# A fused attention and SwiGLU kernel: integer weight conversion in fewer steps, the first batch's attention in token halves, quarter sums used where they are made, and a new order for the first stretch

## The chip, the cores and the metric

The kernel runs on one core of a Trainium2 chip. The metric is the device time of one execution in microseconds (us); the median of several runs is taken.

## The reference

Eight batches of 512 tokens and 32 states of width 512 (8 heads of 64) read each other by attention; the 544 rows of each batch then go through a feed-forward block with RMS norm and gated SiLU.

```python
# x: (8, 8, 512, 64), state: (8, 8, 32, 64), both float32
scores = 1/sqrt(D) * x @ state.T          # (B, H, 512, 32)
xread  = softmax(scores, -1) @ state      # tokens read the states
scores2 = 1/sqrt(D) * state @ x.T         # (B, H, 32, 512)
sread  = softmax(scores2, -1) @ x         # states read the tokens
x = concat(xread, sread)                  # -> rows (B * 544, 512)
xn = x / sqrt(mean(x * x, -1) + 1e-6) * rms_g
g, val = xn @ w_gate, xn @ w_val          # 512 -> 1536
out = (g * sigmoid(g) * val) @ w_out      # 1536 -> 512
```

`moe_rms_g` and the three weights come as they are made by `setup_inputs()`: the weights are float64 (a float32 array times a float64 scalar), so that each value has 8 bytes in the chip's memory and the kernel makes a float32 out of it on the chip.

## The kernel before, in words

**Layout.** Batches run one after the other. Batch 0 works while the weights arrive and is done plainly; batches 1 to 7 use a scheme of seven products for the hidden layer (`hidden_seven`, L842) and, twice nested, for the output (`project_twice`, L1146), whose sums of weights and of quarter weights are made once. The states' rows of all batches come last.

**Weights.** They come in 18 raw pieces of 128 x 1024 doubles (1 MB), three for each of six pairs `mp` of hidden blocks: gate, value and output columns. `load_piece` puts a piece into a buffer of the pool `raws` (4 buffers, `RAW_AHEAD`), by SP's queue; when a piece has been converted, the load of the one four further on is issued. ScalarE makes the exponent of each value in three steps (`exponents`: L246, L249, L252). VectorE makes the mantissa in two (`values`: L273, L276) and multiplies the two in a third (L282), in 1024 columns a step. The first piece is done in two parts. The finished gate and value weights lie in one of three buffers `w_sb` and are stored to memory for later batches (`fetch` brings them back).

**Batch 0's attention.** `first_half` and `second_half` handle 256 tokens each, in two chunks of 128 tokens. The state is transposed (L463) into `apart`, where a head pair has its two heads in separate columns. `chunk_scores` transposes x (L499, four 128x128 transposes a chunk), copies it (L501), makes the scores (L504) and the softmax's maximum, difference and exponential (L510 to L514). `half_read` sums the exponentials (L522), divides, transposes (L532), copies to `aT_s` (L535), multiplies by the state's Gram matrix (`gram`, made at L475 and L479) to get each token's square sum (L543), sums that over partitions by matmuls (L548), takes the power -1/2 on GpSimd (`mean_root`, L299), spreads the result over rows (`along_rows`, L306 and next) and scales `aT_s` (L558). Tokens are read by value weights: `own_weights` (L695) multiplies the scaled state by a pair's weights to `v`, so that the hidden layer of a token is `v` times `aT_s` (`hidden`, L738; two matmuls for each of gate and value, 512 columns). `states_read` with `state_scores` (L568) is the other direction. `project_as_ready` (L945) is the output product of batch 0.

**Batch 1's attention** (`tokens_read`, from L328) begins while batch 0 runs.

**Quarter sums.** `weight_sums` (L988) makes sums of the output weights. `weight_quarters` (L1100) makes of each of seven outer blocks three quarter sums `w2` (pool of three buffers) and one in place, 128 x 384 each, stores them, and `fetch_quarters` brings them back (576 KB) for each use, also for the first one, in batch 1. Four steps a block; blocks 2, 3, 6 in batch 0 (stream Q), 0, 1, 4, 5 in batch 1 (stream q).

**PSUM pools.** `aps`, `vps`, `fx` with two banks each, `fy` and `fz` with one.

**Order.** Each part of the work is a generator that yields after each step. A string names the generators in the order in which their next step is issued; each engine takes its instructions in that order, and semaphores do the rest. `ORDER` (400 letters) is batch 0 with the beginnings of batch 1, `FIRST` is batch 1, `PERIOD` batches 2 to 6, `LAST` batch 7, `STATES` the states' rows. The letters of `ORDER`: a, b the two halves; s the states of batch 0; A, S batch 1's two reads; e exponents, d values; v `own_weights`; h, t, u hidden products, SiLU and gate of batch 0; p, c projection and its stores; w, k, Q first products of batch 1, weight sums, quarter sums; z a matmul on the identity (`keep_awake`, L1281: one call is one matmul of 256 columns, which counts as two instructions), 16 of them, of which most stand in the first 75 letters.

Of the kernel before, what the change touches and what calls it, by code (L numbers as in the profile page):

```python
# [20 lines left out]
RAW_AHEAD = 4  # L21
W_BUFS = 3
FLAT = 1793.0

ORDER = (
    "zzzaaazazbabaaabdebdbadeabeazszbbeadebeezdzbazzaabbaszeabbazzddbebeaaezbddabddsa"
    "eAbzAAdaeasAbAaeAvsavvbaAdsdAdsAhdtdAhehudpdpeedthdeededdevupddvevpddAeehdeddteh"
    "dAAAdeheuAAdeSSedhddpvAtudAdeAAvvpdphhdAshAAteshAueepdetpSedesAeddAdedpsdduddsde"
    "psvevvdedpAhsddeedddtheeeAedehvsvuvAeAhddpddtpAduedpheAAdAedAehdAhtSddSAdevvdvuA"
    "phhtAdheSudAheAtAtdphkkuSkAkkkkuAkSSASkwkpSwQsQwpQppwwpskSQpcQkSQScpcQQwQcwwQwQQ"  # L30
# [10 lines left out]
    "vaaahahatthhqxthaxuqhahutthtxuhquuqhtahqhaauqahluvtvuhhhtquxqqqhttqxuhqxquhxqufx"  # L41
    "hhtahqtuqahhxuthaautsahahuuhtGahtvuauthkaahuxauhuhxtshhuautgxuahkhtuGthtkhuuuhuu"
    "khutppushpuupukapkkkppkkcakpppcpkkfpkkGppagkpppppaapsaakpkpckfpapkfkckasokppaaaa"
    "kpsscskpappapkpgpppgksskagaoppkcagppksaakppkaapwpkpspskskwoxkwxkxppxpfxokglcopsc"
    "foxsoo"
# [14 lines left out]
def kernel(  # L60
# [49 lines left out]
    HS = S // 2  # L110
    QM = HM // 2
# [12 lines left out]
    def load_state(b):  # L124

        rows[b] = two.tile([P, 2, D], F32, name="rows")
        for e in range(2):
            nc.sync.dma_start(out=rows[b][:, e], in_=state[b, e::2])

    def load_x(b, *queues):  # L130
# [5 lines left out]
        x_sb[b] = (one if b else x_0).tile([P, NC, H * D], F32, name="x_b")  # L136
        for c in range(NC):
            (queues or (nc.sync,))[c % max(1, len(queues))].dma_start(
                out=x_sb[b][:, c].rearrange("p (h d) -> p h d", h=H),
                in_=x[b, :, P * c:P * c + P, :].rearrange("h p d -> p h d"))  # L140

    ident = consts.tile([P, P], F32, name="ident")
# [9 lines left out]
    for i, bound in enumerate((-896.0 - 7.5 / 16, 1.0, 255.0 * 128, 1e-6)):  # L152
        GE.memset(bounds[:, i:i + 1], bound)
    rms_g = consts.tile([P, NI], F32, name="rms_g")

    groups = consts.tile([P, 4, Ns], F32, name="groups")
    for i in range(4):
        GE.tensor_copy(groups[:, i], ident[:, 0:Ns])
        for j in range(1, 4):
            GE.tensor_tensor(out=groups[:, i], in0=groups[:, i],  # L160
                             in1=ident[:, Ns * j:Ns * j + Ns], op=ALU.add)


    apart = x_0.tile([P, 4, 2, Ns], F32, name="apart")
    GE.memset(apart, 0.0)
    blocks = x_0.tile([P, P], F32, name="blocks")
    GE.memset(blocks, 0.0)
    for j in range(4):
        GE.memset(blocks[Ns * j:Ns * j + Ns, Ns * j:Ns * j + Ns], 1.0 / DM)
# [10 lines left out]
    for mp in range(NM // 2):  # L180
        for dram in (moe_w_gate, moe_w_val):
            pieces.append(dram[:, 2 * P * mp:2 * P * mp + 2 * P].rearrange("(i p) f -> p i f", p=P))
        pieces.append(
            moe_w_out[2 * P * mp:2 * P * mp + 2 * P].rearrange("(m p) f -> p m f", p=P))
# [12 lines left out]
    def home(k):  # L197

        mp, kind = divmod(k, 3)
        if kind == 2:  # L200
            return wo[:, 2 * mp:2 * mp + 2].rearrange("p m (i f) -> p m i f", f=P)
        return (w_sb[mp] if kind else new_w(mp))[:, :, :, kind, :]

    def load_parts(k):

        src = pieces[k] if k < len(pieces) else None
        if src is None or src.dtype == F32:
            return
        raw[k] = raws.tile([P, 8 * P, 2], I32, name="raw")
        out_ = raw[k].rearrange("p (a f) two -> p a (f two)", a=src.shape[1])  # L210
        for a in parts(k):
            nc.sync.dma_start(out=out_[:, a], in_=src[:, a].bitcast(I32))
# [6 lines left out]
    def parts(k):  # L219

        n = pieces[k].shape[1]
        return (slice(0, n // 2), slice(n // 2, n)) if k == 0 else (slice(0, n),)

    exs = {}

    def columns(k, a):
        n = pieces[k].shape[1]
        return slice(8 * P * a.start // n, 8 * P * a.stop // n)  # L230

    def exponents():
# [3 lines left out]
        for k in range(len(pieces)):  # L236
            for a in parts(k):
                if k not in raw:
                    yield from range(3)
                    continue  # L240
                if a.start == 0:
                    exs[k] = conv.tile([P, 8 * P], I16, name="ex")
                    lin = conv.tile([P, 8 * P], F32, name="lin")
                ex, line = exs[k][:, columns(k, a)], lin[:, columns(k, a)]
                half = raw[k][:, columns(k, a)].bitcast(I16)[:, :, 3::4]
                SE.activation(out=line, in_=half, func=ACTF.Prelu, scale=1.0 / 16,  # L246
                              bias=bounds[:, 0:1], alpha=1.0 / FLAT)
                yield
                SE.activation(out=ex, in_=line, func=ACTF.Prelu, bias=bounds[:, 1:2],  # L249
                              alpha=FLAT)  # L250
                yield
                SE.activation(out=ex.bitcast(U16), in_=ex, func=ACTF.Relu, scale=128.0,  # L252
                              bias=bounds[:, 2:3])
                yield

    def values():
        for k in range(len(pieces)):
            for a in parts(k):
                if a.start == 0:
                    to = home(k)  # L260
                    if k in raw:
                        top_ = conv.tile([P, 8 * P], I32, name="top")
                dst = to[:, a]
                if k not in raw:
                    src = pieces[k].rearrange("p a (c f) -> p a c f", f=P)
                    for i in range(a.start, a.stop):
# [1121 lines left out]
```

## Time and profile before

| | |
|---|---|
| median of 3 runs | 745.59 us (744.95 to 745.7) |
| span of the profiled execution | 742.6 us; of it the profile shows no other total, so the span is its own time, 3.0 us under the median of the runs |
| TensorE (PE) | 735.6 us busy, 5582 matmuls |
| VectorE (DVE) | 579.0 us |
| ScalarE (ACT) | 380.2 us |
| GpSimd (POOL) | 260.3 us |
| DMA | 146.15 MB, mean 197 GB/s |

The profile takes one execution by the hardware's profiler. Busy time is the time in which an engine executed; a share that is near the whole span says that this engine has little idle time left, and where it has any must be looked up by stretch. The chain of waits follows the work that ended last back to the start: each piece begins where the one that released it ended. A row of a group gives line, engine, operation, tiles and shapes, then the number of instructions, the busy time in us, the mean of one in ns, and the idle time of the engine just before them with what ended it.

### The profile page before, as it was taken

What the parts mean: (1) busy time and instruction counts of PE and PEld (TensorE: products, weight loads), DVE (VectorE), ACT (ScalarE), POOL (GpSimd) and SP (SyncE); (2) the same over time, 40 slices, a digit from 0 to 9 for tenths busy, and PEclk for the clock granted to TensorE, in tenths of its full rate; (3) what the DMA queues carried; (4) which work ended last, traced back from release to release, by engine and by line L of the source; (5) the groups of instructions that cost most, each with busy time, mean ns of one, the idle gap of its engine ahead of it and who ended that gap; (6) DMA issues with size and microseconds to landing.
All of it is one profiled execution on the core that took longest, in us unless ns stands there. A gap on an engine that the chain in (4) does not pass through costs nothing.

```text
span 742.6 us, 14225 instructions
## 1 busy us (share of the span) xinstructions
PE 735.6 (99%) x5582; PEld 591.0 (80%) x5582; DVE 579.0 (78%) x957; ACT 380.2 (51%) x635; POOL 260.3 (35%) x362
## 2 busy tenths in 40 slices
PE   8999999999999999999999999999999999999998
PEld 6534444779977998789878997799778987899996
DVE  4999978899856994699659985799469955798862
ACT  5999972573265725472366426562556336511220
POOL 3100004341283128512573228312841267324400
PEclk9999999999999999999999999999999999999999
DMA  9987936964783278608881669328860883063411
GB/s 296 274 294 274 398 118 223 309 245 148 239 304 105 90 285 283 195 1 297 228 304 23 226 213 315 98 95 292 274 188 6 317 230 127 1 223 117 135 52 28
DMA packets 60994, 146.15 MB, mean 197 GB/s; under 512 B 14848, under 2 KB 31744, under 8 KB 54016
## 3 DMA queue, kind: packets, MB, share of 16 engines
q1 hardware_dynamic: 47808, 125.78, 48.9%
q10 hardware_dynamic: 13120, 19.47, 9.2%
q8 instruction: 44, 0.72, 0.4%
q14 instruction: 22, 0.18, 0.1%
HBM read 116.46 MB, written 28.77 MB: 196 GB/s over the span
## 4 chain that ended last, share of the span: by engine, by line
PE 98%; ACT 1%; DMA 1%; DVE 0%; SPq 0%; issue 0%; DVEq 0%
PE f L842 40%; PE f L1146 31%; PE f L945 6%; PE pv L738 6%; PE pv L695 3%; PE at L695 3%; PE f L1008 2%; PE at L631 1%; PE at L355 1%; PE at L437 1%; DMA rows<-in_state_dram 1%; PE f L1281 0%; PE pv L504 0%; PE at L306 0%; PE at L499 0%; PE at L649 0%
## 5 line engine op out<-in xcount | busy, mean ns | idle before, releaser
L842 PE MATMUL f<-aT_s,v 128*128 128x256 f32 x504 | 118.8, 381 | 0.0
L842 PEld LDWEIGHTS f<-aT_s,v 128*128 128x128 f32 x504 | 94.8, 191 | 19.2 <-DVE h L1200 4.2
L905 DVE TENSOR_TENSOR g<-g,f 128x512 f32<-128x512 f32 x84 | 55.8, 684 | 58.6 <-PE f L842 45.7
L842 PE MATMUL f<-aT_t,vs 128*128 128x256 f32 x336 | 86.6, 381 | 0.0
L1174 POOL TENSOR_TENSOR kept<-kept 128x256 f32<-128x256 f32 x28 | 20.9, 746 | 183.2 <-DVE kept L1186 116.9
L1159 ACT COPY kept<-f 128x512 f32<-128x512 f32 (+1 forms) x56 | 30.1, 538 | 105.8 <-PE f L1146 99.8
L1146 PE MATMUL f<-w,h 128*128 128x128 f32 x588 | 74.7, 276 | 0.0
L842 PEld LDWEIGHTS f<-aT_t,vs 128*128 128x128 f32 x336 | 63.0, 190 | 12.5 <-issue 3.5
L1146 PEld LDWEIGHTS f<-w,h 128*128 128x128 f32 x588 | 69.8, 192 | 1.1 <-DVE h L1200 0.8
L722 POOL TENSOR_TENSOR vs<-v 128x256 f32<-128x256 f32 x42 | 31.0, 737 | 109.8 <-ACT v L707 109.6
L896 ACT ACTIVATE hb<-g 128x1024 f32<-128x1024 f32 x42 | 44.4, 1058 | 46.8 <-DVE g L905 43.1
L299 POOL TENSOR_TENSOR ri<-ss,mhalf 128x4 f32<-128x4 f32 (+1 forms) x9 | 9.4, 1045 | 126.9 <-issue 82.0
L918 DVE TENSOR_TENSOR hb<-hb,f 128x512 f32<-128x512 f32 (+1 forms) x48 | 31.1, 649 | 28.8 <-PE f L842 28.7
L945 PE MATMUL f<-wo,hb 128*128 128x512 f32 x96 | 44.0, 599 | 0.0
L738 PE MATMUL pv<-aT_s,v 128*128 128x512 f32 x96 | 43.8, 598 | 0.0
L842 PE MATMUL f<-aT_t,v 128*128 128x256 f32 x168 | 43.8, 383 | 0.0
L842 PE MATMUL f<-aT_s,vs 128*128 128x256 f32 x168 | 43.3, 380 | 0.0
L1146 PE MATMUL f<-wo,h 128*128 128x128 f32 x336 | 42.3, 275 | 0.0
L1146 PE MATMUL f<-wo,hb 128*128 128x128 f32 x336 | 42.1, 275 | 0.0
L918 DVE TENSOR_TENSOR hb<-hb,c 128x512 f32<-128x512 f32 (+1 forms) x48 | 35.7, 743 | 6.5 <-ACT hb L896 6.1
L1146 PEld LDWEIGHTS f<-wo,hb 128*128 128x128 f32 x336 | 40.3, 192 | 0.4
L1146 PEld LDWEIGHTS f<-wo,h 128*128 128x128 f32 x336 | 39.8, 192 | 0.0
(227 smaller groups left out, 1639.9 us busy)
## 6 DMA issues: line engine op xcount, KB each, us to landing
w_m<-w_d SPq DMA_DIRECT2D x48, 1024.0 KB
w<-t_d SPq DMA_DIRECT2D x49, 576.0 KB
out_dram<-kept SPq DMA_DIRECT2D x28, 256.0 KB
raw<-in_moe_w_val_dram SPq DMA_DIRECT2D x6, 1024.0 KB
raw<-in_moe_w_out_dram SPq DMA_DIRECT2D x6, 1024.0 KB
w_d<-w_m SPq DMA_DIRECT2D x6, 1024.0 KB
x_b<-in_x_dram SPq DMA_DIRECT2D x6, 1024.0 KB
x_d<-xB ACTq DMA_DIRECT2D x6, 1024.0 KB
```

Of the source, the lines that this page charges most:

```text
L695: TE.matmul(out=pv[e][Ns * j:Ns * j + Ns, :], lhsT=stT_g[b][D * e:D * e + D, j, :], rhs=w[D * e:D * e + D, j].rearrange("p m k f -> p (m k ...
L722: GE.tensor_tensor(out=vs[:, 0], in0=a21, in1=a22, op=ALU.add)
L738: TE.matmul(out=to[0], lhsT=lhs(i, k), rhs=r, start=(i == 0), stop=(i == len(rhs) - 1))
L842: TE.matmul(out=ps[:, i, 0:half], lhsT=l[:, i, :], rhs=r, start=(start and i == 0 and k == 0), stop=(k == len(lhs) - 1), skip_group_check= ...
L896: SE.activation(out=hb[:, 2 * mp:2 * mp + 2, 0:n].rearrange("p m (c t) -> p m c t", c=2), in_=q["g"][:, :, :, 0:half], func=ACTF.Silu if s ...
L905: VE.tensor_tensor(out=to, in0=to, in1=q[ps][:, :, 0:half], op=ALU.add)
L918: VE.tensor_tensor(out=part, in0=part, in1=val, op=ALU.mult)
L945: TE.matmul(out=banks[r], lhsT=hb[:, m, P * r:P * r + P], rhs=wo[:, m, :], start=(m == 0), stop=(m == NM - 1))
L1008: TE.matmul(out=banks[name][:, r, :], lhsT=lhs(k)[:, P * r:P * r + P], rhs=rhs(k), start=(start and r == 0 and k == 0), stop=(k == HM - 1) ...
L1146: TE.matmul(out=to[half][:, slot, :], lhsT=lhs[:, k, :], rhs=rhs[:, k, :], start=(fresh and n in (0, 4) and k == 0), stop=(k == QM - 1), s ...
L1159: SE.copy(of_half(k, i), banks[name][i])
L1174: GE.tensor_tensor(out=k[:, 4:8:3], in0=k[:, 5:6].to_broadcast([P, 2, QD]), in1=k[:, 4:8:3], op=ALU.add)
```

## The change

**Weights as integers.** A raw piece lands 2 bytes behind a word boundary of its tile (`I16` tile with one more double). One 32-bit word then holds the middle of a double: sign, exponent and top of the mantissa come as one 16-bit half, and the rest of what float32 needs lies in one word. ScalarE takes two steps, and gives the sign and exponent bits and the mantissa's top as an int32 (`tops`); VectorE takes two: one `tensor_scalar` (multiply and minimum) on the words, and one bitwise OR that writes the float32's bits. For `mp` 0 the first two pieces hold gate and value of one hidden block each instead of gate of two and value of two. `RAW_AHEAD` is 5.

**Batch 0's attention.** Its x comes in two halves of 256 tokens, two neighbouring tokens on a partition (`load_x_halves`), and its output is stored accordingly. The scores use a wider `apart`; the state is transposed twice, with the head pair swapped the second time. The exponentials are transposed before the division. The matrix `gram` has four more columns that sum the exponentials, so that one matmul gives squares and sums, tokens on partitions; L548 and `along_rows` go from here, and a second set of transposes comes. `of_states` (letter g) makes the state's Gram matrix and scaled state; `rms_g` is loaded as four rows and transposed. `first_own` makes `v` of the first pair of hidden blocks in two parts, and `first_pair` does their hidden products in two halves of 256 tokens.

**Quarter sums.** `early_quarters` (Q, blocks 0 to 2) and `late_quarters` (q, blocks 3 to 6) leave the sums in the buffers from which batch 1 uses them; the seven loads for batch 1 go.

**Order.** `ORDER` has 352 letters and 11 keep-awake steps (z 6, y 5; they run on `wake`, a tile of ones that VectorE fills); `FIRST` is new. The sums `groups` are a stream of their own (i).

```diff
-RAW_AHEAD = 4
+RAW_AHEAD = 5
...
 ORDER = (
-    "zzzaaazazbabaaabdebdbadeabeazszbbeadebeezdzbazzaabbaszeabbazzddbebeaaezbddabddsa"
-    "eAbzAAdaeasAbAaeAvsavvbaAdsdAdsAhdtdAhehudpdpeedthdeededdevupddvevpddAeehdeddteh"
...
+    "zyzaaiayaigaeeaeaaagdaadeddgggzzzbbbbbbaaabzdbeyaaabegvvbabiyayaaebvddaevbavvaae"
+    "bbesbshAhbbdAbbeddsdebbiAAAAhtdvvhvAAhstuudeAthAAsesdsAApsppAApseeeAAAAAeuAhstee"
...
+    def load_x_halves():
+        x_sb[0] = x_0.tile([P, 2, H, HT, D], F32, name="x_b")
+        for i in range(2):
+            for h in (slice(0, H // 2), slice(H // 2, H)) if i == 0 else (slice(0, H),):
+                nc.sync.dma_start(out=x_sb[0][:, i, h].rearrange("p h c d -> p h (c d)"),
+                                in_=x[0, h, HS * i:HS * i + HS, :].rearrange("h (p c) d -> p h (c d)", c=HT))
+            yield
...
     def load_parts(k):
-        raw[k] = raws.tile([P, 8 * P, 2], I32, name="raw")
...
+        raw[k] = raws.tile([P, 8 * P + 1, 4], I16, name="raw")
+        flat = raw[k].rearrange("p f four -> p (f four)")[:, 1:1 + 32 * P]
+        out_ = flat.rearrange("p (n f) -> p n f", n=len(pieces[k]))
...
     def exponents():
-                SE.activation(out=line, in_=half, func=ACTF.Prelu, scale=1.0 / 16,
-                              bias=bounds[:, 0:1], alpha=1.0 / FLAT)
-                SE.activation(out=ex, in_=line, func=ACTF.Prelu, bias=bounds[:, 1:2],
-                              alpha=FLAT)
-                SE.activation(out=ex.bitcast(U16), in_=ex, func=ACTF.Relu, scale=128.0,
-                              bias=bounds[:, 2:3])
+                SE.activation(out=lin[:, c], in_=raw[k][:, c.start + 1:c.stop + 1, 0], func=ACTF.Prelu,
+                              bias=bounds[:, 0:1], alpha=1.0 / FLAT)
+                SE.activation(out=tops[k][:, c], in_=lin[:, c], func=ACTF.Prelu, scale=2.0 ** 19,
+                              bias=bounds[:, 1:2], alpha=FLAT)
...
     def values():
-                    VE.tensor_scalar(top, hi, 0xfffff, 0x100000,
-                                     op0=ALU.bitwise_and, op1=ALU.bitwise_or)
-                    VE.scalar_tensor_tensor(out=man, in0=top, scalar=2.0 ** 32,
-                                            in1=r.bitcast(U32)[:, :, 0], op0=ALU.mult, op1=ALU.add)
-                    VE.scalar_tensor_tensor(out=dst, in0=man, scalar=-2.0 ** -52, in1=ex,
-                                            op0=ALU.mult, op1=ALU.mult)
+                    VE.tensor_scalar(rest, word, 2.0 ** -13, 2.0 ** 19 - 1, op0=ALU.mult, op1=ALU.min)
+                    VE.tensor_tensor(out=dst.bitcast(I32), in0=rest, in1=top, op=ALU.bitwise_or)
...
     def half_read(h):
+        yield from transposed()
+        ge = [f.tile([P, 2, P + 4], F32, name="f") for f in (fy, fz)]
+        for c in range(HT):
+            for i in range(2):
+                TE.matmul(out=ge[c][:, i, :], lhsT=aT[:, i, P * c:P * c + P], rhs=gram[:, i, :],
+                          start=True, stop=True)
...
+        VE.tensor_tensor(out=e, in0=e, in1=z2.rearrange("p c k -> p (c k)").unsqueeze(2).to_broadcast(e.shape),
                          op=ALU.mult)
+        yield from transposed()
...
+    def early_quarters():
+        for o in range(3):
+            yield from quarter_weights(o)
+            nc.sync.dma_start(out=t2_d[o], in_=w2_sb[o])
+            yield
+            if o != 1:
+                yield from last_quarter(o)
...
     def fetches_of_quarters(b):
-        for n in range(7 * (b - 1) + 3, 7 * b + 3):
+        for n in range(7 * (b - 1) + 3 if b > 1 else 7, 7 * b + 3):
...
+    def first_pair():
+        for i in range(2):
+            for m in range(2):
+                for k in range(2):
+                    for e in range(2):
+                        TE.matmul(out=done_[m][k][:, HS * i:HS * i + HS], lhsT=v_sb[0, 0][0][:, e, m, k, :],
+                                  rhs=aT_s[0][:, e, HS * i:HS * i + HS],
+                                  start=(i == 0 and e == 0), stop=(i == 1 and e == 1), skip_group_check=True)
+                yield
...
-    load_x(0, nc.scalar, nc.scalar, nc.sync, nc.sync)
+    nc.scalar.dma_start(out=rms_rows, in_=moe_rms_g.rearrange("(i p) -> i p", p=P))
+    first_x = load_x_halves()
+    next(first_x)
     load_piece(0)
-    load_piece(1)
-    nc.sync.dma_start(out=rms_g, in_=moe_rms_g.rearrange("(i p) -> p i", p=P))
-    for k in range(2, RAW_AHEAD):
+    next(first_x, None)
+    for k in range(1, RAW_AHEAD):
         load_piece(k)
     load_state(1)
     load_x(1)
```

More of the change, by code (lines that the diff above doesn't have):

```diff
@@ L261, in values @@
                     if k in raw:
[L262 removed]
+                        words = raw[k].rearrange("p f four -> p (f four)").bitcast(U32)
+                        words = words[:, 0:16 * P].rearrange("p (f two) -> p f two", two=2)[:, :, 1]
                 dst = to[:, a]
                 if k not in raw:
[L265 to L267 removed]
```

355 lines of the change are left out of this document (210 added, 145 removed).

## The prediction, on record before the changed kernel ran

> **What bounds the kernel now.** I read the page first (busy times), then the chain that ended last, in order of time, then busy times by stretch and the groups of the first 130 us.
>
> ```profile
> span 742.6 us, 14225 instructions
> PE 735.6 (99%) x5582; PEld 591.0 (80%) x5582; DVE 579.0 (78%) x957; ACT 380.2 (51%) x635; POOL 260.3 (35%) x362
> ```
>
> TensorE is busy 99% of the span: the other 7.0 us (742.6 - 735.6) are all that it is idle. So only two things can move the time: less work on TensorE, or fewer moments in which it waits or runs fillers. The next question is where those moments are. The chain in order of time, from its first matmul, and then from the first product of batch 0 (L738) on:
>
> ```profile
> 5.64 0.45 PE at L463
> 6.09 0.85 PE f L1281 x2
> 6.94 0.85 PE at L499 x4
> ...
> 9.50 0.96 PE pv L504 x8
> 10.46 0.44 PE at L499 x4
> ...
> 13.97 0.49 PE f L1281 x2
> 14.46 1.02 PE at L568 x16
> ...
> 17.50 0.49 DVE gram L479 x2
> ...
> 20.09 0.59 ACT aT_s L535
> ...
> 25.04 0.69 DVE eS L543
> ...
> 25.78 1.05 PE f L548 x8
> 26.83 0.27 PE pv L306 x2
> 27.10 0.44 PE at L328 x4
> 27.54 1.02 PE f L695 x16
> ```
>
> ```profile
> 29.87 5.41 PE pv L738 x12
> 35.28 3.43 PE f L945 x8
> ...
> 41.45 3.63 PE f L945 x8
> ...
> 129.62 11.37 PE f L842 x52
> ```
>
> From 29.87 on each piece starts where the one before it ends: 12 + 8 matmuls of 512 columns at 0.43 us, the next, and so on into batch 1. The 0.20 us by which 3.63 exceeds 3.43 follows a packed group (L695, 64x32 tiles; an earlier one stands at 27.54); it is a change of tile shape, not a wait for data. So nothing behind 29.87 waits, and all that can be won in waits lies ahead of it. There the chain passes through VectorE and ScalarE (softmax, norm) and through fillers (L1281, the keep-awake matmuls, 16 steps in the order string). The matrix engine also starts at half pace: four transposes (L499) take 0.85 us at 6.94 and 0.44 us at 10.46.
>
> The other engines in the first stretch, and in batch 1 (128 to 172 hidden products, 172 to 210 projection):
>
> ```profile
> 0.00:100.00 100.00, 96.68 (x492) 48.83 (x493) 83.14 (x121) 89.65 (x113) 8.18 (x37) 1.00 0.86 296
> 128.00:172.00 44.00, 43.95 (x278) 33.90 (x259) 40.59 (x71) 26.75 (x46) 16.49 (x20) 1.00 0.72 246
> 172.00:210.00 38.00, 38.00 (x419) 34.42 (x418) 31.75 (x55) 12.79 (x28) 14.01 (x18) 1.00 0.66 224
> ```
>
> (Columns: length, then busy PE, PEld, DVE, ACT, POOL, granted clock, DMA share, GB/s.) ScalarE at 89.65 of 100 us and the DMA engines at 0.86 are nearly full in the first 100 us; yet they don't hold TensorE up there.
>
> **The change, part by part.**
>
> *Weights as integers.* Per piece of 1024 columns, from the groups of the first 130 us:
>
> ```profile
> L246 ACT ACTIVATE lin<-raw,bounds 128x1024 f32<-128x1024 int16 x17 | 21.2, 1244 | 0.0
> L249 ACT ACTIVATE ex<-lin,bounds 128x1024 int16<-128x1024 f32 x17 | 19.6, 1150 | 0.2
> L252 ACT ACTIVATE ex<-ex,bounds 128x1024 uint16<-128x1024 int16 x17 | 19.5, 1149 | 0.2
> L276 DVE SCALAR_TENSOR_TENSOR raw<-top,raw 128x1024 f32<-128x1024 int32 x17 | 20.8, 1221 | 0.2
> L273 DVE TENSOR_SCALAR top<-raw 128x1024 int32<-128x1024 int32 x17 | 11.6, 682 | 0.0
> ```
>
> ScalarE goes from 1.24 + 1.15 + 1.15 to 1.24 + 1.15: 1.15 less, 18 pieces, 20.7 us. VectorE now takes 0.68 (L273) and two steps of two inputs, 1.22 each (L276; L282 is of the same kind and size); the change leaves a tensor_scalar and an OR of two tensors. The OR has two inputs like L276, so 1.22. The tensor_scalar multiplies and clips 32-bit integers, which no row does; its bounds are 0.68 (L273, one input, same size and stride) and 1.22 (L276). I take 0.68, the same kind of instruction: 1.22 less, 22 us. Both savings fall behind 29.87, where TensorE does not wait: worth nothing there. Ahead of it they shorten two queues, and that is inside the chain below.
>
> *Landing two bytes off.* The raw weights land 2 bytes past a word, so that one 32-bit word holds the middle of each double. No row shows such a transfer; it may cost nothing (a gain has no cause, for the bytes and descriptors are the same) or much. The point from which it costs: in 0 to 100 the DMA share is 0.86, so 14 us are free; the 18.9 MB of weights at 296/0.86 = 344 GB/s are 55 us of that. It may be 14/55, a quarter, slower before the stretch is bound by DMA. I take nothing. The Trainium skill, page "DMA: Bandwidth & Descriptors", section "How a descriptor splits into AXI transactions", says that a run that doesn't start on 256 bytes takes one transaction more; by it a 2 KB row would take 9 for 8, an estimated 12%, and the sum would stay as it is. No run of this kernel shows it.
>
> *Attention of batch 0 in halves.* TensorE loses the sums over partitions (L548, 2 x 1.05) and the rows of the norm (L306, twice 0.27): 2.6. It gains a second set of transposes (8 at 0.11, 0.9), the second state transpose and the one of rms_g (0.2), a second start of the split first product (L695 in halves of 256 columns, 0.2) and of the state scores, which now share tiles (L568, 1.02, some 0.2 more), and eight half-width gram products per half, at L548's 0.13 a matmul, for two of 256 columns (0.2). Some 0.9 less in all.
>
> The path to the first hidden product, from rows: the state's load is now alone at the head of the queues, so I let the first transposes start at 5.6 instead of 6.94 (bound on the other side: 6.4, if the state lands as now). Two groups at the slow 0.85: 7.3. The copy with its drain (0.8) and sixteen score matmuls (0.96 for eight): 10.0. Maximum and subtraction at 0.69 would end at 11.6, but the exponential queues on ScalarE behind the copies of half 1, whose transposes stand behind a Gram product (four of 128 columns, 0.44), the transpose of rms_g (0.1) and three fillers (0.49 each): 12.0. With two groups of transposes (0.88), drain, copy (0.59), the exponential (0.62) and 0.3 for handing over it ends at 14.6. Now the exponential ends at 15.4, as the first of these rows shows (the second is the norm's power on GpSimd):
>
> ```profile
> 14.74 0.62 ACT L514 ACTIVATE eS<-eS 128x512 f32<-128x512 f32 x1
> L299 POOL TENSOR_TENSOR ri<-ss,mhalf 128x2 f32<-128x2 f32 x2 | 2.3, 1139 | 18.8 <-DVE ss L552 17.3 <-ACT lin L246 1.5
> ```
>
> so 0.8 is gained up to there. Then: transposes 0.44 + 0.2 of drain, copy 0.59, Gram with drain 1.2, two products of 256 columns at 0.42 (between 0.25 for 128, L479, and 0.69 for 512, L543), small ones 0.6 (two, each about half of L479's 0.49), reduction 0.69, small ones 0.5, power and product on GpSimd 1.25 (the power alone has a mean of 1.14), 0.8 behind the other half's product in VectorE's queue, norm 0.69, transposes 0.64, copy 0.59 + 0.3 behind v's copies, the state scores 1.2: 10.5, and 0.5 for a filler that waits on its bank. 14.6 + 11.0 = 25.6, against 29.87: **4.3 earlier**.
>
> Of TensorE's work some is not done earlier but later: batch 1's transposes (L328: 16 at 0.11, and its state's two, 0.2) and the second half's last four (0.44) now come behind the first product: **2.4 later**. All lighter work named above lies ahead of it, inside the path. One change of tile shape more: 0.2.
>
> *First half of the hidden products.* first_pair splits two pairs into 256 columns: as many columns; L842 runs that shape at 11.37/52 = 0.219, half of 0.43 and a little: 0.1 more over 32. It hides the wait for half 1's norm.
>
> *The queues.* On SP's queue x of batch 0 now comes in two halves with piece 0 between them, then pieces 1 to 4, then batch 1's state and x; one piece more (1 MB, 3.0 us at 344 GB/s) stands in front of the latter, whose first user, batch 1's transposes, comes behind the first product. On GpSimd the group sums (L160) stand behind the state's copy now, and nobody waits for them before batch 1.
>
> *Quarter sums where made.* Seven loads of 576 KB go; at a DMA share of 0.66 they were hidden. But 16 of batch 1's sums move from the hidden products into the projection:
>
> ```profile
> L1100 DVE TENSOR_TENSOR wo<-wo x4: 546/552/552, 138.2 to 150.5; 128x384 f32<-128x384 f32 x4
> ```
>
> 16 x 0.55 = 8.8 on top of 31.75 in 38 us would be too much; the new string takes four steps of batch 2's reading (0.69 each, 2.7) ahead of the projection, which leaves 37.9 of 38. I take nothing for it, and it is the third rival.
>
> *Sum.* -4.3 + 2.4 + 0.2 + 0.1 = -1.6; span 741.0. The median of the runs lies 745.59 - 742.6 = 3.0 above the span: **744.0**, 0.2% faster. With the start at 6.4 it is 0.8 more; without the queueing terms (0.8, 0.5, 0.3) 1.6 less.
>
> **The rivals.**
>
> *The front closes further.* If the new order string matches the chip better than my chain, the fillers fall where they cost nothing: three fillers and the 1.6 of queueing, 1.5 + 1.6 = 3.1 off, 740.9. For it: 16 fillers become 11. Against it: each stands in front of a wait in the new string too.
>
> *The tensor_scalar at one element a cycle.* 0.54 more a piece; the two halves and two pieces ahead of the first product make 0.54 x 3 = 1.6: 745.6, no change. Later pieces still take 2.44 for 3.12 now.
>
> *VectorE full in batch 1's projection (slower).* The place is 172 to 210. A product of seven steps takes
>
> ```profile
> 172.16 14.07 PE f L1146 x126
> ```
>
> 42 x 0.112 = 4.7. There are three buffers for quarter sums, so the sums of the fourth may start only when the first product is done, and VectorE takes its queue in order: what stands behind them, the sums that the projection itself needs, waits too. Once VectorE is over 0.1 us late (38.0 - 37.9) TensorE waits; the price is up to one product: 744.0 + 4.7 = 748.7. Against it: VectorE has 44 - (40.59 - 8.8 + 2.7) = 9.5 us in hand before 172.
>
> *The landing.* At half more time per raw transfer, 55/2 - 14 = 13.5: 757.5.
>
> *The clock.* The half pace ends at about 9.3 now, though the clock column reads 1.00. If it ends 3 us later, the second eight scores (0.96) and half the Gram product (0.24) take twice as long: 1.2 more, 745.2. The Trainium skill, page "TensorE: Matmul & The Clock Gate", section "Part 1: The HAM clock gate", says that the clock opens after a busy window of about 3.4 us, of free phase, and closes after an idle one. The two L499 rows agree with it; by that rule the fillers that are left out in the first 5 us can shift the opening by one window.
>
> **How the numbers follow.** Over 0.2% (1.5 us, about what a measurement of this kernel tells from no change: its three runs lie 0.75 apart) faster is what most of the forecast's own spread (742.4 to 744.8) and the first rival give. Chances: forecast 0.42 (half of it within 0.2%), the front closing further 0.24, tensor_scalar 0.06, clock 0.06, VectorE 0.12, landing 0.05, other delays of the new string 0.05. Faster 0.24 + 0.23 = 0.47; same 0.19 + 0.06 + 0.06 = 0.31; slower 0.22. Range: down to 740.1 for the first rival (740.9 less the 0.8 of the start), up to 748.7 for VectorE; the landing and the extremes are left out. The forecast's own range is 742.4 to 744.8.
>
> **What would show it.** First hidden product near 25.6 and no gap on TensorE behind it; ScalarE's two steps on weights at 21.2 and 19.6 us as now and the third gone, VectorE's OR at 1.22 and tensor_scalar at 0.68; no reload of quarter sums in batch 1. I am wrong if the chain leaves TensorE after 30 us (towards raw loads: the landing; towards quarter sums at 180 to 200: VectorE), or if the first product starts after 28 or before 24.

## The result, and the profile after

The changed kernel takes 748.89 us (median of five, 746.23 to 749.92) where the kernel before, run beside it, takes 745.59 (744.27 to 746.5). The ratio is 1.0044 with a 95% interval of 1.0025 to 1.0063: it is slower, by more than the 0.2% that can be told from no change. The forecast was 744.0, and 748.89 lies just above the end of the range, 748.7, and the time moved the other way.

The profiled execution was the shortest of the five, 746.23 us with a span of 744.2. Its page, first the span and the busy times:

```profile
span 744.2 us, 14282 instructions
PE 734.0 (99%) x5618; PEld 591.0 (79%) x5618; DVE 562.9 (76%) x954; ACT 365.0 (49%) x624; POOL 265.1 (36%) x364
```

TensorE's work is down by 1.6 us (735.6 to 734.0), VectorE's by 16, ScalarE's by 15, and yet the span is 1.6 longer: TensorE is idle for 10.2 us in place of 7.0. The timeline of TensorE shows when the first hidden product starts, 24.89 against 29.87:

```profile
24.89 1.99 PE L1361 MATMUL pv<-aT_s,v 128*128 128x256 f32 x8
```

So the front does what it was to do, and the time is lost later. It gains this by lighter work and not by fewer waits: in the first 30 us TensorE is idle for 3.73 us in place of 3.32, and the filler matmuls there take 8.1 us in place of 11.0. The waits of TensorE from 30 us on (a view that is empty for the kernel before), and its busy time by stretch (columns as in the prediction):

```profile
PE f L906 <- ACT g L953: 1.1, 1, 1.1
PE f L1228 <- DVE h L1278: 1.0, 1, 1.0
PE at L695 <- DVE sr L690: 0.5, 1, 0.5
PE at L347 <- ACT aT_s L563: 0.2, 1, 0.2
```

```profile
0.00:30.00 30.00, 26.27 (x195) 19.05 (x196) 18.83 (x52) 21.06 (x33) 11.24 (x39) 1.00 0.93 276
30.00:130.00 100.00, 99.44 (x533) 44.59 (x540) 70.00 (x106) 64.76 (x91) 12.74 (x13) 1.00 0.76 284
140.00:145.00 5.00, 3.95 (x19) 3.16 (x18) 2.49 (x4) 2.99 (x5) 2.37 (x3) 1.00 0.84 192
172.00:210.00 38.00, 36.89 (x395) 33.62 (x394) 37.79 (x64) 10.54 (x25) 12.30 (x13) 1.00 0.44 143
```

Before, TensorE was idle for 3.32 us in the first 30 (26.68 busy) and for nothing in the other three. Now it is idle for 3.73 + 0.56 + 1.05 + 1.11 = 6.45. That is 3.1 us more idle time for 1.6 less work: a net 1.5, and the last matmul ends at 740.53 for 739.01.

Three waits, three places: 119 us, 144 us, and 188 to 208 us (the 0.2 at L347 ends at 30 us, within the front). For the one at 144 the chain in order of time says what TensorE waits for:

```profile
126.68 0.47 DVE wt L1168
127.15 2.41 DVE xB L357 x4
129.56 0.02 issue
129.58 10.23 DMA x_d<-xB
...
139.88 0.34 ACTq L364
...
142.47 0.95 ACT hb L960
143.43 0.48 ACT g L953
143.91 0.14 issue
144.04 3.69 PE f L906 x16
```

Read backwards: the matmuls wait for the gate copy `g`; it stands in ScalarE's queue behind `hb`, and that behind the issue of the load `xG` (L364), which cannot be issued until the store `x_d` has landed. The store takes 10.23 us. Before, it ran from 132.46 to 139.88, 7.4 us. It starts 2.9 us earlier than before and lands at the same time, while TensorE comes there 2.6 us earlier (batch 1's first product at 126.83 for 129.46).

Why it takes longer is in the timeline of SP's DMA queue, before and then after:

```profile
128.63 0.33 SPq L195 DMA_DIRECT2D w_m<-w_d  x1
...
129.91 6.97 SPq L1102 DMA_DIRECT2D t_d<-w  x2
...
142.21 4.47 SPq L1102 DMA_DIRECT2D t_d<-w  x2
146.78 0.38 SPq L195 DMA_DIRECT2D w_m<-w_d  x1
```

```profile
129.95 20.11 SPq L221 DMA_DIRECT2D w_m<-w_d  x3
```

Before, the stores of quarter sums (`t_d`), which wait for sums that VectorE hasn't made yet, stood in that queue between the 1 MB fetches of weights and kept the second one back until 146.78. The change moves these stores, and the fetches run ahead into the time of the store `x_d`. What the DMA engines moved from the store's issue to its landing, before (132.46 to 139.88) and after (129.58 to 139.81), has the store as the 1.05 MB of the second row (ScalarE's queue), and beside it, in the first row, what SP's queue moved:

```profile
q1 hardware_dynamic: 446, 1.61, 59.0%
q10 hardware_dynamic: 528, 1.05, 36.7%
```

```profile
q1 hardware_dynamic: 581, 2.15, 57.0%
q10 hardware_dynamic: 528, 1.05, 34.3%
```

Before, the store was not alone either: the quarter sums' own stores ran beside it. After, two fetches take their place: it is 0.54 MB more, and in all 3.23 MB pass in 10.23 us where 2.69 passed in 7.42. Why the pace is lower too is not shown.

### The profile page after: what moved, and what is told of

The parts are those of the page before. It is cut to its first block, busy times and chain, and to the rows that moved or that the text cites. A ratio compares the mean times of both kernels' runs of the same rounds, so it can differ in the third digit from the quotient of the medians.

```text
span 744.2 us, 14282 instructions
## 1 busy us (share of the span) xinstructions
PE 734.0 (99%) x5618; PEld 591.0 (79%) x5618; DVE 562.9 (76%) x954; ACT 365.0 (49%) x624; POOL 265.1 (36%) x364
## 4 chain that ended last, share of the span: by engine, by line
PE 87%; DVE 8%; DMA 2%; ACT 1%; issue 1%; POOL 0%; ACTq 0%; SPq 0%; DVEq 0%
PE f L906 37%; PE f L1228 27%; PE pv L802 5%; PE f L1009 4%; PE pv L740 3%; PE f L1072 2%; PE at L740 2%; DVE w L1162 1%; DMA x_d<-xB 1%; PE at L676 1%; PE at L374 1%; PE at L456 1%; PE pv L536 1%; DVE h L1280 1%; DVE h L1282 1%
## 5 line engine op out<-in xcount | busy, mean ns | idle before, releaser
L958 ACT COPY g<-f 128x512 f32<-128x512 f32 x42 | 24.8, 591 | 25.8 <-PE f L906 24.1
```

Source lines behind the costliest of these rows:

```text
L958: SE.copy(gates(q)[1], q["x"][:, :, 0:half])
```

## The experiments

The theory after this reading: (1) the x_d store, slowed by fetches that nothing holds back any more and started late by VectorE's order, blocks ScalarE's queue. Rivals: (2) VectorE is full in batch 1's projection; (3) the landing of the raw weights two bytes off a word costs transfer time; (4) the end of the program, after the last matmul, takes longer. "Before" is each time the kernel before, run beside it on the same chip (medians 744.35 to 745.08).

**The two halves of the change.** after_again is the changed kernel once more. front_only has the new weights and the new front, with the old quarter sums and the old `FIRST`; quarters_only has the old front and weights, with the new quarter sums and the new `FIRST`.

```diff
 # front_only, against the changed kernel
-    "...SpvQhwSpQQQuhwwhwtwhtSShkwkkukkQQkukQQQSppSkwkQkQppQkpSckpQccQc"
+    "...SpvhwSpuhwwhwtwhtSShkwkkukkkukSppSkwkkQQpQpQkQpQSQcQkQpQcQcQc"
-    "Q": early_quarters()          # FIRST and q likewise
+    "Q": weight_quarters(VE, 2, 3, 6)
```

> The changed kernel once more, as the measure of the others. Both theories: 748.9 us. The first profile caught an execution of 744.2 us span, the other four had 746.6 to 747.9. Theory A (batch 1 pays: VectorE is full there, and the store of batch 2's transposed x holds ScalarE's queue): a profile of a usual execution has the 2.7 us more as waits of TensorE between 127 and 212. Theory B (the front and the weights pay): the 2.7 us lie before 127.

> The changed front, weights and first-stretch order, but the quarter sums and batch 1's order string as before (stored, then loaded again; 12 sums at the end of batch 0, 16 in batch 1). Theory A: the front's gain stays and batch 1 has no gap: batch 1 begins 2.6 us earlier, 743 to 744.5 us, less than before's 745.6. Theory B: about 749, as the changed kernel.

> The kernel before with the new quarter sums and batch 1's new order string alone. Theory A: VectorE at 9.7 or more of each 10 us from 150 to 210, TensorE waits 2.5 to 5.5 us there, 748 to 751 us. Theory B: 745.6 as before, or a little less for the seven loads that go.

after_again 748.7, 1.0057 [1.0037, 1.0077]; front_only 745.67, 1.0015 [1.0003, 1.0027]; quarters_only 754.57, 1.0139 [1.0118, 1.0161]. The loss belongs to the quarter sums and their order: front_only loses 1.0 us, the changed kernel 4.0, quarters_only 9.9. Two expectations missed: front_only gains nothing on the kernel before, and the long wait of quarters_only does not lie between 150 and 210. In quarters_only the chain shows the store at its longest, and the stretches what the long wait does to the clock:

```profile
131.62 15.47 DMA x_d<-xB
...
151.12 6.25 PE f L843 x16
```

```profile
145.00:150.00 5.00, 0.00 (x0) 0.00 (x0) 0.00 (x0) 1.53 (x3) 0.38 (x1) 0.95 0.46 127
150.00:155.00 5.00, 3.88 (x9) 3.19 (x10) 1.78 (x3) 2.05 (x4) 2.89 (x4) 0.50 0.57 113
```

The wait is 6.2 us, and the sixteen matmuls behind it take 6.25 for 3.69, since the granted clock is 0.50. Beside this store SP's queue moved 4.23 MB (131.62 to 147.09), four times the store:

```profile
q1 hardware_dynamic: 1076, 4.23, 71.8%
```

Two fetches issued at 132.50 are half of it; the rest was issued just ahead of the store (a fetch at 128.54, two stores of quarter sums, and an output store).

**Moving the load, moving the fetches.** late_xG moves three of the four issues of `xG` four ScalarE steps later in `FIRST` (late_xG_all does it in `PERIOD` too). late_fetch leaves them and issues the two fetches on ScalarE's queue behind `xG` (their letters f move up in `FIRST`). sums_out is late_xG with the twelve late quarter sums left out and loads of earlier stored ones in their place.

```diff
 # late_xG, FIRST
-    "haahaaavtvhaattxhhuuhuhxhtthtxhhhtqhuhahuuaauxxttauhhuuthtu...
+    "haahaaavtvhaattxhhuuhuhxhtthtxhhhtqhuhhuuuxxttaaaauhhuuthtu...
 # late_fetch
-            nc.sync.dma_start(out=new_w(n), in_=w_d[n % (NM // 2)])
+            (queue or nc.sync).dma_start(out=new_w(n), in_=w_d[n % (NM // 2)])   # nc.scalar for n = 11, 12
 # sums_out
-            yield from quarter_weights(o)
+            nc.sync.dma_start(out=w2, in_=t2_d[o % 3])
```

> The changed kernel; in batch 1's order string three of the four issues of the load of batch 2's transposed x (ScalarE's queue, L364) go four ScalarE steps later, to the fourth. Theory X (that queue waits there for the store of x, and two copies and a SiLU stand behind it, which TensorE needs): the 1.1 to 1.7 us wait at 144 goes and with it the slow clock that follows a longer one: 745 to 746.5 us, granted clock 1.00. Theory V (VectorE, full from 150 to 210, sets the end): what is won at 144 is waited for behind 150 again, 748 to 749.

> The changed kernel; the two 1 MB fetches of weights that run beside the store of batch 2's x are issued on ScalarE's queue behind the loads of x instead of by SP's queue at 130. Theory X, part 2 (the store takes 10.2 to 10.9 us for 7.4 because of them): the store takes 7 to 8 us, the wait at 144 goes, 745 to 746.5. If the store's time does not depend on them: 748 to 749 and 10 us or more again.

> late_xG, and 12 of the 17 late quarter sums are left out (the three tiles of blocks 3 to 6 are loaded from the stored ones of blocks 0 to 2 instead, so the values of these blocks are others): 6.6 us less on VectorE between 180 and 210. Theory V: 3 us or more faster than late_xG. Theory X: only the 1.0 us wait at 190 and the 0.1 at 208 go, about 1 us faster than late_xG.

> late_xG with the same move in the string of batches 2 to 6 too. Theory X: in batch 2 the queue waits for the store in some executions; 744 to 746 us and a narrower spread than late_xG. Theory V: as late_xG.

late_xG 747.88, 1.0049 [1.003, 1.0068]; late_xG_all 748.61, 1.0047 [1.0031, 1.0063]; late_fetch 746.64, 1.0026 [1.001, 1.0043]; sums_out 752.92, 1.0115 [1.0096, 1.0135]. Issuing the load later frees `g`, but then the load itself is late: TensorE waits 0.9 us at L374, and the chain of late_xG has

```profile
143.41 5.74 DMA xG<-x_d
```

late_fetch has no wait at 144. Its stretch 135 to 140, after that of the changed kernel:

```profile
135.00:140.00 5.00, 5.00 (x25) 4.40 (x24) 3.93 (x6) 2.06 (x4) 1.67 (x2) 1.00 0.90 363
```

```profile
135.00:140.00 5.00, 5.00 (x25) 4.41 (x24) 4.00 (x5) 2.81 (x5) 2.33 (x3) 1.00 0.09 10
```

The DMA share falls from 0.90 to 0.09: without the two fetches the store, issued at 130.23, is through by about 135, with 0.11 MB of SP's queue beside it. So the fetches are what makes it long in the changed kernel. The profile of late_fetch has 4.9 us behind the last matmul for 3.7 in the changed kernel's, so that the last matmul ends only 0.6 us sooner than there (739.9 for 740.53) and the span is no shorter. sums_out decides nothing: its extra loads at 184 to 190 fill the DMA engines and bring a wait of their own,

```profile
PE at L676 <- DMA e<-e_d: 4.8, 1, 4.8
```

**The store's length, the sums' length.** after_short, front_short and before_short store only a quarter of `x_d`, and the loads read that quarter; sums_short makes the late sums over 32 of 128 columns and fills the rest with zeros on GpSimd.

```diff
 # after_short, front_short, before_short
-            nc.scalar.dma_start(out=x_d[b % 2].rearrange("q g f r -> (g f) q r"), ...
+            nc.scalar.dma_start(out=x_d[b % 2][0:1].rearrange("q g f r -> (g f) q r"), ...
 # sums_short
+        if o > 2:
+            GE.memset(w2[:, :, :, 32:QD], 0.0)
-            VE.tensor_tensor(out=to, in0=a, in1=b, op=ALU.subtract)
+            VE.tensor_tensor(out=to[:, :, 0:n], in0=a[:, :, 0:n], in1=b[:, :, 0:n], op=ALU.subtract)  # n = 32
```

> The changed kernel with the round trip of the transposed x through memory made cheap in batches 2 to 7: only a quarter of it (256 KB for 1 MB) is stored, and the four loads read that quarter (three quarters of the scores' x are then another head's). Theory S (the round trip is what makes the changed kernel slow, beside the VectorE waits of 1.5 us that its traces show at 119 and 190): the store takes 3 us or less for 10, no wait at 144, 744.5 to 745.5 us. Theory V (VectorE): 748 or more, as the changed kernel.

> The same cut in the kernel before. Its trace has no wait of TensorE on the round trip: 744 to 745 us, as the kernel before or up to 0.5 us less (executions in which the store was slow). By Theory S the distance of the changed kernel to this one, 4 us without the cut, shrinks to 0.5 to 1.

> The same cut in front_only (new front, old quarter sums and old string of batch 1). Theory S (what the front gains is lost at the round trips of batch 1 and 2: 0.7 and 2.2 us of waits in its trace): 742.5 to 743.5, 1.2 us or more under before_short. If the front gains nothing: 744.5 to 745.5, as before_short.

> The changed kernel; the 12 late quarter sums are made over 32 of 128 columns only, the rest is filled by GpSimd with zeros (so these blocks' products are others): some 0.3 us less VectorE for each, 3.6 us between 180 and 210. Theory V: the waits at 190 and 208 go, VectorE under 9.5 of 10 there, 1 us or more faster than the changed kernel: 747 or less. Theory S: at most those 1.1 us.

after_short 745.87, 1.0017 [1.0008, 1.0027]; before_short 744.53, 1.0 [0.9987, 1.0014]; front_short 745.94, 1.002 [1.0008, 1.0032]; sums_short 747.88, 1.0047 [1.0035, 1.0059]. A short store takes about 2.8 us from the changed kernel (748.7 to 745.87) and nothing from the kernel before or from front_only, where 742.5 to 743.5 had been expected. In after_short the store also starts 1.8 us earlier (127.78 for 129.58), chiefly since it needs only the first of the four transposes. Shorter sums take the waits at 190 and 208 away (0.2 left), but the median stays within the interval of the changed kernel's. Its profile caught a longer wait at 144 than the changed kernel's own:

```profile
129.73 11.65 DMA x_d<-xB
...
145.45 5.38 PE f L906 x16
```

```profile
145.00:150.00 5.00, 4.55 (x13) 3.75 (x14) 2.46 (x4) 1.38 (x3) 2.30 (x3) 0.66 0.42 84
```

Here TensorE waits 2.3 us, and the clock at half costs 1.7 more (5.38 for 3.69). (Another wait at `g`, of 0.9 us, lies at 550 to 560 us in this profile, far from there.) This also tells why the medians of the changed kernel lie above its profiled execution: the store takes 10.2, 10.9 and 11.65 us in three profiles of that code or nearly that code, the wait is 1.1, 1.7 and 2.3, and in the third the clock adds its part.

**Code loading and the landing.** On the page of the changed kernel the queue that loads instructions has 45 packets, before 44; but on that of after_again, the same code, it is 44 too, so the count alone says little. before_pad and front_pad add 40 and 52 tiny matmuls early, in front_pad in place of two fillers, so that the load near the end falls elsewhere. on_the_word lands the raw weights on a word boundary.

```diff
 # before_pad, front_pad
+        for i in range(calls):
+            TE.matmul(out=ps[...], lhsT=src[:, 0:Ns], rhs=src[:, 0:64], start=True, stop=True)
 # on_the_word
-        flat = raw[k].rearrange("p f four -> p (f four)")[:, 1:1 + 32 * P]
+        flat = raw[k].rearrange("p f four -> p (f four)")[:, 0:32 * P]
-                SE.activation(out=lin[:, c], in_=raw[k][:, c.start + 1:c.stop + 1, 0], func=ACTF.Prelu,
+                SE.activation(out=lin[:, c], in_=raw[k][:, c.start:c.stop, 3], func=ACTF.Prelu,
```

There is no time of the same landing without the second pair of lines (aligned): ScalarE would read a value of the tile that nothing has written.

> The kernel before with 40 more matmul instructions (a 32x64 tile, 0.016 us each) in TensorE's first wait, so that its program is as long as the changed kernel's (5622 for 5618 matmuls, 5582 before). Theory T (a code load more, 45 of 16 KB for 44, lands within 4 us of the last stores and holds them up by 1.3 us; seen in front_only, front_short, late_fetch, after_short): 45 loads, from the last matmul to the end of the span 4.9 us for 3.6, 745.5 to 746 us. Without T: 744.6, as before.

> front_only with 52 more matmul instructions in the first wait (for two keep-awake steps), which moves the last code load some 6 us ahead of the end. Theory T: 3.6 us from the last matmul to the end, 743.5 to 744.5 us, under the kernel before. Without T: 745.7, as front_only.

> The changed kernel with the raw weights landing on a word, not 2 bytes behind it (the words read are then other bits, so the weights made are others, by the same instructions and bytes). The landing theory: the front or the transfers get faster, 747.5 or less. Theories S and T: no difference, 748 to 749.

before_pad 744.58, 1.001 [0.9994, 1.0025]; front_pad 745.61, 1.0015 [1.0003, 1.0027]; on_the_word 751.81, 1.0102 [1.0083, 1.0122]. From the last matmul to the end of the span it is 5.2 us in before_pad's profile, where a load of instructions follows the last matmul within about 1 us, and 3.6 in that of the kernel before; in front_pad's profile it is 3.9 where front_only's had 5.3. So it is in all twenty profiles: the eight with such a load 1.0 to 1.7 us behind the last matmul end 4.9 to 5.3 us after it, the other twelve 3.6 to 3.9, and the changed kernel is one of the twelve (3.7), so that the tail is no part of its loss there. The tail is there in the profiles, but the medians of the padded kernels do not follow it: rival 4 is not shown by the times, and stays open for the versions with the long tail. on_the_word is no clean test of rival 3: its groups show a new tie between ScalarE and VectorE, which now work on the same word,

```profile
L273 ACT ACTIVATE lin<-raw,bounds 128x1024 f32<-128x1024 int16 x17 | 21.1, 1243 | 3.6 <-DVE raw L298 3.6
L298 DVE TENSOR_SCALAR raw<-raw 128x1024 int32<-128x1024 uint32 x17 | 11.7, 688 | 3.9 <-ACT lin L273 3.9
```

but its transfers can be compared: from the records of the single packets in the first 100 us, one of 2048 bytes took 86.0 ns on average there, 87.0 in the changed kernel and 93.1 in the kernel before; one of 4096 bytes 184.7, 188.9 and 165.9. Between landing on the word and two bytes off lie 1 to 2%, and so the landing costs next to nothing. (The 4096-byte packets take longer than before in both, so that isn't the landing.)

**VectorE's order.** early_sums takes the changed kernel and only moves letters k and Q ahead of the gate steps u near the end of `ORDER`, among themselves in the same order; front_early does the same to front_only. early_late adds late_fetch to early_sums, front_early_pad the tiny matmuls to front_early.

```diff
 # early_sums, end of ORDER
-    "...SpvQhwSpQQQuhwwhwtwhtSShkwkkukkQQkukQQQSppSkwkQkQppQkpSckpQccQc"
+    "...SpvQhwSpQQQkkkuhwwhwtwhtSShwkkQQkukQQQkkQuSppSwkQppQkpSckpQccQc"
```

> The changed kernel with the weight and quarter sums at the end of batch 0 (letters k and Q) one group earlier on VectorE, each ahead of the gate step (u) that waits 1.8 to 2.3 us for TensorE there, in the same order among themselves. Theory S, cause (the sums stand between that wait and the transposes of batch 2's x, so that its store starts at 130 and meets the fetches): the transposes come 3 us or more ahead of 127, the store lands before 137, no waits at 119 and 144: 745 to 746 us. If the store only takes longer by as much: 748 to 749.

> early_sums and late_fetch together. Theory S: like early_sums or up to 0.5 us less, the VectorE wait of 1.0 us at 190 is left: 744.5 to 745.5.

> front_only (old quarter sums) with its sums moved forward in the same way. If the 0.7 us of waits on VectorE and GpSimd at 130 to 140 and the random ones behind are what the front loses: 744 to 745, at or under the kernel before. If the front gains nothing for another reason: 745.6 again.

> front_early, whose trace has no wait behind 30 us and its last matmul 1.3 us before that of the kernel before, but 5.1 us from there to the end for 3.6; with the 52 short matmul instructions of front_pad, which take the last code load away from the end. Theory T: 3.6 to 3.9 us to the end, 743 to 744 us, 0.1 to 0.2% under the kernel before. Without T: 744.6, as front_early, at the kernel before.

early_sums 744.95, 1.0013 [0.9998, 1.0028]; early_late 746.2, 1.0021 [1.0008, 1.0034]; front_early 744.63, 0.9998 [0.9982, 1.0013]; front_early_pad 744.25, 1.0009 [0.9991, 1.0027]. Moving those letters alone takes the changed kernel from 1.0057 to 1.0013. The timeline of VectorE in early_sums, and TensorE's waits from 30 us on:

```profile
122.47 1.08 DVE L1168 TENSOR_TENSOR wt<-wt 128x384 f32<-128x384 f32 x1
123.47 2.48 DVE L357 STREAM_TRANSPOSE xB<-x_b 128x512 f32<-128x512 f32 x4
```

```profile
PE f L1228 <- DVE h L1278: 1.0, 1, 1.0
...
```

The transposes of batch 2's x start at 123.47 for 127.06, the store is issued at 127.53, and ScalarE issues `xG` at 137.38 without waiting: the waits at 119 and 144 are gone, and the 1.0 at 190 stays. Two fetches still run beside the store (from 129.42); it has time enough now. In early_late the fetches have nothing left to free, and the run gains nothing over early_sums: the waits from 30 us on are the same, its median is 1.25 us higher, and its profile has 5.0 us behind the last matmul for 3.7, which would account for that but is not shown to. In front_early only the 0.2 is left of the waits; the last product in its chain, and in that of the kernel before, is

```profile
734.89 2.82 PE f L1072 x13
```

```profile
734.89 4.12 PE f L1008 x19
```

so TensorE is done 1.3 us sooner (734.89 + 2.82 = 737.71 for 739.01). Its span is 742.8 all the same, with 5.1 us behind the last matmul for 3.6, and its median equals that of the kernel before. No version here is shown to beat it.

## Why the prediction was wrong

**What held.** The front: its first transposes start at 5.49 where 5.6 was taken, the first half's exponential ends at 13.90 for 14.6, the first product starts at 24.89 for 25.6, and with the later waits taken away (front_early) the last matmul ends 1.3 us sooner, where the sum gave 1.6. The weights as integers: two steps on ScalarE and VectorE's two, as priced (0.68 and 1.22), from the groups of the first 130 us:

```profile
L273 ACT ACTIVATE lin<-raw,bounds 128x1024 f32<-128x1024 int16 x17 | 21.3, 1251 | 0.0
L276 ACT ACTIVATE ex<-lin,bounds 128x1024 int32<-128x1024 f32 x17 | 19.7, 1156 | 0.3
L302 DVE TENSOR_TENSOR w_m<-raw,ex 128x1024 int32<-128x1024 int32 x11 | 13.5, 1225 | 2.1 <-ACT ex L276 1.4
L298 DVE TENSOR_SCALAR raw<-raw 128x1024 int32<-128x1024 uint32 x17 | 11.7, 687 | 0.0
```

Per piece that is 1.14 us less on ScalarE and 1.21 on VectorE, and behind the front it moves no work of TensorE, as argued. The landing was taken at nothing and costs next to nothing. The Trainium skill, page "DMA: Bandwidth & Descriptors", section "How a descriptor splits into AXI transactions", would have made such rows an estimated 12% dearer; measured are 87.0 ns against 86.0, 1.2%.

**The step that failed** is "Quarter sums where made", with "The queues" beside it: "Seven loads of 576 KB go; at a DMA share of 0.66 they were hidden", "I take nothing for it". Transfers were counted by their load on the DMA engines, and not by their place in SP's queue. The prediction's part on the queues follows x and the state of batch 1 past what is new in front of them, but doesn't ask what the moved stores had stood in front of. What stood behind them were the weight fetches: the second one came forward from 146.78 into the time of the store `x_d`, which then took 10 to 12 us for 7.4, with ScalarE's whole queue behind its landing. late_fetch shows this by taking the fetches away. VectorE's order at the end of batch 0 is the other side of the same race, and the prediction prices sums only in batch 1: the new string has sums behind gate steps, which wait for TensorE, and batch 2's transposes behind the sums. This did not make the store late against the kernel before (it starts 2.9 us earlier, TensorE comes 2.6 us earlier), but it left no room for a longer one. early_sums starts it 2.1 us earlier still, and gives back 0.44% (1.0057 to 1.0013), some 3.3 us. Either one removes the wait at 144; only early_sums removes the 0.5 at 119 too, and both together gain nothing over it.

**"So nothing behind 29.87 waits, and all that can be won in waits lies ahead of it"** was right and not enough: where nothing waits there can still be something to lose. In the kernel before, the store landed at 139.88 and TensorE had work until ScalarE's next copies were done. With TensorE 2.6 us ahead and the landing where it was, 1.1 us of that was missing: the slack was about 1.5 us (2.6 - 1.1, an estimate), and no step looked for it.

**The rival "VectorE full in batch 1's projection"** named a place, 172 to 210, where VectorE is indeed full (37.79 of 38 us) and TensorE waits. In the chain, just ahead of that wait:

```profile
187.56 1.00 DVE h L1276
188.56 0.47 DVE wt L1168
189.03 0.47 DVE w L1162
189.50 0.47 DVE h L1278
```

The sum `h` that TensorE needs stands behind two quarter sums. The size was off: 1.1 us and no product of 4.7. And its share of the loss is the smaller one, for early_sums keeps this wait and stands at 1.0013. That its 748.7 agrees with the measured median is luck.

**The median.** "The median of the runs lies 745.59 - 742.6 = 3.0 above the span" was carried over as a constant. Only 1.8 to 2.1 of it is one, in every profiled execution (746.23 and 744.2, 749.35 and 747.5): the rest is how far the profiled execution lies from the others. It was 0.9 before (3.0 - 2.1, an estimate, for the time of that profiled execution is not on record) and is 748.89 - 746.23 = 2.7 after, for a wait that is a race between a store and TensorE differs from run to run.

**Open.** front_only's 1.0015 is not accounted for. front_early stands at 0.9998, but the waits at `g` and `c` in the profile of front_only (1.8 + 0.5 + 0.4) don't explain it: that execution, 748.17 us, is the longest of its twelve, and the 1.8 and 0.4 lie between 210 and 300 us, in batch 2, where the moved letters have no step. Only the 0.5, with 0.2 more on GpSimd at 130 to 140, lies where they act. And the 1.3 us that TensorE gains in front_early do not reach the median. The longer tail takes them in its profile; whether it does so in every execution was not settled by the padded kernels.

## What to carry to other kernels

When a transfer leaves a queue, ask what it stood in front of: that starts earlier from then on, and its new neighbours are the price, however idle the DMA engines are on average. When an engine gets ahead, look along its next few microseconds for the events that do not move with it (a store's landing, a step late in another engine's order), and take their slack from the trace before, where they show no wait. And compare a profiled execution with its own time before carrying its distance to the median over to another kernel.

## What was not expected of the hardware

- The same 1 MB store took under 5 us with 0.11 MB of SP's queue beside it (late_fetch), 7.4 beside 1.61 MB (before), 10.2 beside 2.15 (the changed kernel) and 15.47 beside 4.23 (quarters_only).
- TensorE's clock fell to half after a single wait of 2.3 us (sums_short: 0.66 over the 5 us, 5.38 us for 3.69), and not after one of 1.7 (granted clock 1.00 from 145 to 150 in after_again). The Trainium skill, page "TensorE: Matmul & The Clock Gate", section "Part 1: The HAM clock gate", has the clock close after an idle window of about 3.4 us; the 6.2 us of quarters_only agree, and the 2.3 of sums_short closed it sooner than that.
- The last two stores are issued by ScalarE's queue in 0.85 us in the profile of the kernel before, and in 2.26 in that of front_early, which has a load of instructions at 738 to 739 us, just then. Moving such a load into that place (before_pad) or out of it (front_pad, front_early_pad) moved the profile's tail with it, by 1.2 to 1.6 us, but not the medians; whether the loads make it in every execution is open.
- A 128x384 sum on VectorE takes 0.47 us in most of the projection (the rows above) and 1.0 in several places where GpSimd is at work beside it: L1276 above, and the sums at the end of batch 0, which take 1.0 while GpSimd is busy (116.0 to 124.3) and 0.56 right behind. That the one slows the other is argued from these times alone.
